# Gates of two chunks at a time by seven products of halves, from chunk 6 on

## The chip, the core and the metric

The kernel runs on one core of a Trainium2 chip. The metric is the device time of one execution in microseconds (us). The engines of the core are TensorE (PE, matmuls into PSUM; PEld is its loading of weights), VectorE (DVE), ScalarE (ACT), GpSimd (POOL) and SyncE (SP, which only issues DMAs here).

## What is computed

Linear attention with random features, and behind it a bilinear feed-forward layer on all 4608 tokens:

```
proj = q_s @ omega.T ; h = proj - |q_s|^2 / 2        # the same for k
q_p, k_p = exp(h - max(h)) / sqrt(m)                  # 128 features a head
kv = sum_s k_p^T v ; z = sum_s k_p                    # a batch and a head
x  = (q_p @ kv) / (q_p . z + 1e-6)                    # 4608 tokens x 512
out = ((x @ w1) * (x @ w2)) @ w3 @ w_out              # w1, w2 512 x 1024; w3 1024 x 1024; w_out 1024 x 512
```

All inputs are float32; 8 batches, 8 heads, 576 tokens a batch, head size 64.

## The kernel before

Tokens go in 36 chunks of 128. For each chunk the kernel makes k's features (`k_chunk`), q's features (`q_chunk`), q's attention (`q_attend`, whose result `xs` holds 128 tokens x 512), the transposed tokens for the gates (`x_turn`), the gates (`gate`) and the output (`project_out`). w3 and w_out are multiplied into one matrix `W` at the start (`W_block`), so the output is one product of the gated values with `W`.

Precision is kept by parts: a float32 operand is split into a high and a low fp16 half (`split`: ACT writes the high one, DVE or POOL the low one), and a product is the three passes high-high, high-low, low-high (`PASSES`). The first chunks are an exception: k and v of chunks below `VF` stay fp32 and are multiplied in one pass (`kv_batch`). The exponentials of q's features come in two forms, chosen by chunk in `DQ`: '1' takes eight ACT operations of one head each, with the maximum as their bias; '0' takes one DVE addition of 128 x 1024 and one ACT operation.

A gate (`gate`, lines 1191 to 1243) takes two chunks (256 tokens) from `GROUPS` on; the first four chunks go one by one. For each of 8 tiles of 128 of the 1024 columns it makes x @ w1 and x @ w2, each as 4 blocks of the 512 rows x 3 passes = 12 matmuls whose moving operand has 256 columns (128 for single chunks). Two tiles share a PSUM bank (`bank_m`, tag `pm`, 4 banks). ACT reads the first factor out (`asb`), DVE multiplies it with the second, ACT casts the high half into `big` and POOL makes the low half. The three pairs of chunks 28 to 33 (`LATE`) have another form behind the gate: `W` is cut into quarters, sums of quarters are mixed beforehand (`mix`, lines 1261 to 1301), DVE sums the gated parts, and `pair_first` and `pair_rest` make the output by seven products in place of eight.

What sets the order: all operations are recorded, in the order in which the code issues them, and then placed by a list scheduler (`Plan`), which knows each operation's inputs and outputs, a cost for each (`cost`, line 322), the buffers of a tag, and that POOL and DVE keep each other from SBUF in some forms (`locks`). It tries several rankings and keeps the best. Each engine then runs its own operations in the planned order, waiting on semaphores. PE operations of one bank and one kind are joined to groups of at most 24 matmuls (`JOIN`). Where the plan leaves PE idle in the first 200 us, `fill` puts matmuls on `ones_bf` that nobody reads.

Of the kernel before, what the change touches and what calls it, by code (L numbers as in the profile page):

```python
# [39 lines left out]
DQ = '1'  # L40
QF = 6
KF = 11
VF = 7
# [4 lines left out]
WADD = 1  # L48
# [12 lines left out]
LATE = 28  # L61
LATE_END = 34
MIX_N = 3
MIX_E = 'd'
SUM_E = 'd'
LO_E = 'p'
# [23 lines left out]
O_BUFS = 2  # L90
RAW_BUFS = 2
ASB_BUFS = 2
BIGS = 4
MAGS = 4
# [156 lines left out]
class Plan:  # L251
# [9 lines left out]
    def record(self, lane, method, args, kwargs):  # L261
# [15 lines left out]
        )  # L277
        if join:
# [43 lines left out]
    def cost(self, op):  # L322
# [20 lines left out]
        if op.lane == "vector":  # L343
# [5 lines left out]
            elif op.method == "tensor_reduce" or len(wide) > 1:  # L349
                t = 72 + 1.1 * m + (60 if thin else 0)  # L350
# [3 lines left out]
        if op.lane == "scalar":  # L354
            t = (130 if thin else 60) + 0.9 * m + (60 if "accum_out" in op.kwargs else 0)
# [3 lines left out]
        elif op.method == "tensor_tensor":  # L359
            t = 95 + 2.0 * m  # L360
# [119 lines left out]
    def order(self):  # L480
# [16 lines left out]
        plain = {o: set(o.deps) for o in ops}  # L497
        scale = TURN0
        for n in range(ROUNDS):
            start, total, slot = self.forward(rank, plain, turned(plain), costs, True, scale=scale)  # L500
# [3 lines left out]
            for m in range(INNER + 1):  # L504
# [3 lines left out]
                if best is None or total < best[0]:  # L508
                    best = total, start, slot
# [10 lines left out]
        _, start, slot = best  # L520
# [49 lines left out]
ROOM = {"big": 2050}  # L570
# [7 lines left out]
LOCK = True  # L578
HOP = 80
ROUNDS = 2  # L580
INNER = 2
# [4 lines left out]
def tile_favor_attention_then_bilinear_ffn(  # L586
# [35 lines left out]
    def early(kind, fn):  # L622
        return fn
# [53 lines left out]
    def power_of_two(cols, n, name, pre=1.0, add=False, bufs=4):  # L677
# [4 lines left out]
        if add:  # L682
            total = small("total")
# [120 lines left out]
    def features(c, name, e=None):  # L804
# [9 lines left out]
        def project(first=None):  # L814
            for i in range(NP):
                if whole(c, name):
                    for g in range(2):
                        d = slice(g * D, (g + 1) * D)
                        nc.tensor.matmul(
                            pg[:, g, i], raw[d, i], om_raw[d], start=first is None, stop=True  # L820
                        )
                    continue
                for n, (x, y) in enumerate(PASSES):
                    for g in range(2):
# [5 lines left out]
                            start=first is None and n == 0,  # L830
# [6 lines left out]
        nm = small("nm", H)  # L837
# [4 lines left out]
        if kind == "2":  # L842

            project(lambda h: nm[:, h : h + 1].broadcast_to([P, M]))
            nc.scalar.activation(e, pj, AF.Exp, scale=es, bias=ln_e)
        elif kind == "1":
# [106 lines left out]
    def q_attend(c):  # L953
# [7 lines left out]
        for h in range(H):  # L961
# [10 lines left out]
        gd = small("gd", H)  # L972
# [3 lines left out]
        gr = small("gr", H)  # L976
        nc.vector.reciprocal(gr, gd)
        xs = at.tile([P, HD], F32, tag="xs", name=f"xs_{c}", bufs=1)
        nc.vector.tensor_tensor(
            xs.rearrange("p (g i d) -> p g i d", g=2, d=D),  # L980
# [4 lines left out]
        mx = small("mx")  # L985
        nc.vector.tensor_reduce(mx, xs, AX.X, ALU.max, apply_absolute_value=True)
        xss[c] = xs, mx, owners

    def x_turn(c):

        xs, mx, owners = xss.pop(c)
        nc.vector.tensor_scalar(mx, mx, TINY, 2.0**-12, ALU.max, ALU.mult)
        p, r = pow2(mx, 1, f"x{c}")

        pt = sm.tile([P, 1], F32, tag="pt", name=f"pt_{c}", bufs=14)
        for b, r0, r1 in owners:
            nc.vector.tensor_scalar(pt[r0:r1], p[r0:r1], pv[b][r0:r1], None, ALU.mult)
        pts[c] = pt
        t = at.tile([P, 2, HD], F16, tag="xhl", name=f"xhl_{c}", bufs=1)
# [29 lines left out]
    for i in range(TOPS):  # L1029
        t = const.tile([P, 1024], F32, name=f"top_{i}")  # L1030
# [62 lines left out]
    def w12_split(n, i):  # L1093

        l1m = small("l1m")
# [4 lines left out]
        s = small("ws")  # L1100
# [23 lines left out]
    def W_block(n):  # L1124
# [8 lines left out]
        def product():  # L1133
            w = w3c[0].rearrange("p (j i) -> p j i", j=HALF)
            for k in range(2):
                ps = bank_m(f"wp_{n}_{k}")
                if j0 and not WADD:
                    nc.tensor.matmul(ps, ident, Wb[:, i + k + 1], start=True, stop=False)
                for j in range(HALF):
# [4 lines left out]
                        start=j == (0 if WADD else j0),  # L1144
# [46 lines left out]
    def gate(c0, n, u):  # L1191
# [20 lines left out]
        if LATE <= c0 < LATE_END:  # L1212
            g = at.tile([P, 8, P], F32, tag="ek", name=f"g_{c0}_{u}", bufs=EK_BUFS)
            asb = g[:, 0:4].rearrange("p b s -> p (b s)").rearrange("p (f s) -> p f s", f=nf)
            nc.scalar.mul(asb, ab[0], 2.0**-39)
            nc.vector.tensor_tensor(asb, ab[1], asb, ALU.mult)
            by = engine(SUM_E, u)
            by.tensor_tensor(
# [350 lines left out]
```

## Time and profile before

| | us |
|---|---|
| median of 3 runs (780.41 to 781.48) | 780.99 |
| the profiled execution | 780.73 |
| its span, first to last instruction | 779.0 |
| PE busy | 768.9 |
| DVE busy | 512.5 |
| ACT busy | 504.5 |
| POOL busy | 231.5 |

The mean granted PE clock is 0.997 of full speed. Busy time is the time covered by at least one of an engine's instructions. Matmuls are pipelined, so one lasts longer than the distance to the next one: from the start of a group to the start of the group behind it is the better measure of what it costs. Line numbers are of no help in this kernel, since one helper (line 173) issues everything; groups are told apart by the names of tiles and by shapes. `xT` are transposed tokens, `w12b` the split w1 and w2, `Wb` the output matrix, `big` the gated parts, `asb` gate values on the way, `hl` split q and k, `ek`/`eq` features, `vhl` split v, `mag` scratch.

### The profile page before, as it was taken

How to read it: one execution, taken by the hardware profiler on the slowest of the kernel's cores; microseconds unless marked ns; L12 is line 12 of the kernel's file. 1: busy time of each engine (PE TensorE's matmuls, PEld its weight loads, DVE VectorE, ACT ScalarE, POOL GpSimd, SP SyncE). 2: the span in 40 equal slices, each digit the busy share in tenths (PEclk: the TensorE clock that was granted, in tenths of full speed). 3: DMA queues.
4: the chain of work that ended last, by engine and by line, in shares of the span. 5: the costliest groups of instructions: out<-in, count | busy, mean ns of one | idle time of the engine just before them, and what ended most of it. 6: DMA issues, size and time to landing. Idle time of an engine off the chain costs nothing.

```text
span 779.0 us, 20533 instructions
## 1 busy us (share of the span) xinstructions
PE 768.9 (99%) x8525; PEld 591.0 (76%) x8533; DVE 512.5 (66%) x1093; ACT 504.5 (65%) x1038; POOL 231.5 (30%) x210
## 2 busy tenths in 40 slices
PE   9999999998999999999999999999999999999998
PEld 5456589877787777777777777777777777788886
DVE  4357989999764866676667666586668555865311
ACT  5899889756673858668666676587566546444221
POOL 1000020414252434324342334234432433433110
PEclk9999999999999999999999999999999999999999
DMA  9998983324533364263454435164442333322101
GB/s 332 364 308 304 195 169 64 83 56 123 123 83 69 66 179 93 60 162 83 83 102 130 96 83 115 41 149 97 74 101 49 76 80 72 69 42 69 41 2 55
DMA packets 142621, 88.43 MB, mean 114 GB/s; under 512 B 116736, under 2 KB 117120, under 8 KB 142528
## 3 DMA queue, kind: packets, MB, share of 16 engines
q1 hardware_dynamic: 142016, 86.07, 44.9%
q8 instruction: 67, 1.10, 0.6%
q10 hardware_dynamic: 432, 0.79, 0.3%
q14 instruction: 26, 0.21, 0.1%
q0 software_dynamic: 80, 0.26, 0.1%
HBM read 49.35 MB, written 9.44 MB: 75 GB/s over the span
## 4 chain that ended last, share of the span: by engine, by line
PE 87%; DVE 8%; ACT 3%; issue 1%; ACTq 0%; DVEq 0%
PE pm L173 73%; PE pa L173 14%; DVE mag L173 2%; ACT e L173 1%; DVE s_nm L173 1%; DVE Wb L173 1%; DVE w12b L173 1%; DVE vhl L173 1%; DVE hl L173 1%; ACT top L173 0%; ACT junk L173 0%; DVE ek L173 0%; DVE asb L173 0%; DVE xhl L173 0%; DVE xs L173 0%
## 5 line engine op out<-in xcount | busy, mean ns | idle before, releaser
L173 PE MATMUL pm<-xT,w12b 128*128 128x256 f16 (+1 forms) x3840 | 391.5, 262 | 0.4 <-DVE s_es L173 0.4
L173 PEld LDWEIGHTS <-w12b 128*128 128x128 f16 x3840 | 339.1, 98 | 38.1 <-issue 0.5
L173 PE MATMUL pm<-Wb,big 128*128 128x512 f16 (+1 forms) x852 | 173.9, 361 | 0.0
L173 PEld LDWEIGHTS <-big 128*128 128x128 f16 x996 | 95.9, 98 | 80.2 <-issue 1.6
L173 DVE TENSOR_REDUCE s_nm<-pa 128x8 f32<-128x1024 f32 x72 | 86.7, 1219 | 79.0 <-PE pa L173 78.5
L173 POOL TENSOR_TENSOR eq<-e,eq 128x1024 f16<-128x1024 f32 x31 | 67.5, 2177 | 197.1 <-issue 85.8
L173 POOL TENSOR_TENSOR big<-asb,big 128x512 f16<-128x512 f32 x60 | 78.0, 1299 | 160.5 <-ACT big L173 157.4
L173 ACT ACTIVATE e<-pa,s_nm,s_es 128x128 f32<-128x128 f32 x240 | 87.4, 468 | 30.7 <-DVE s_nm L173 19.5
L173 POOL TENSOR_TENSOR ek<-e,ek 128x1024 f16<-128x1024 f32 x26 | 56.4, 2169 | 56.2 <-ACT ek L173 45.5
L173 DVE TENSOR_TENSOR asb<-pm,asb 128x512 f32<-128x512 f32 x60 | 41.2, 686 | 45.7 <-PE pm L173 44.3
L173 ACT CAST big<-asb 128x512 f16<-128x512 f32 x60 | 37.7, 628 | 44.9 <-DVE asb L173 44.8
L173 ACT ACTIVATE o<-pm,oscs 128x512 f32<-128x512 f32 (+1 forms) x31 | 21.0, 676 | 64.0 <-PE pm L173 63.9
L173 PE MATMUL pm<-mag,mag 128*128 128x512 f32 x128 | 57.4, 598 | 0.4 <-DVE mag L173 0.4
L173 ACT ACTIVATE asb<-pm 128x512 f32<-128x512 f32 x60 | 36.2, 604 | 24.1 <-PE pm L173 22.7
L173 PE MATMUL pa<-om,hl 64*128 64x128 f16 x1320 | 44.3, 218 | 3.7 <-DVE hl L173 2.3
L173 PEld LDWEIGHTS <-hl 64*128 64x128 f16 x1320 | 37.4, 95 | 13.0 <-issue 8.2
L173 PEld LDWEIGHTS pm<-mag,mag 128*128 128x128 f32 x128 | 23.6, 190 | 27.0 <-issue 25.6
L173 DVE SCALAR_TENSOR_TENSOR xhl<-xs,s_p2r,xhl 128x512 f16<-128x512 f32 x36 | 32.3, 897 | 17.4 <-ACT xhl L173 17.2
L173 PE MATMUL pa<-vhl,ek 128*128 128x65 f16 (+1 forms) x896 | 43.2, 205 | 0.1
L173 DVE CAST eq<-e 128x1024 f16<-128x1024 f32 x30 | 21.0, 699 | 29.7 <-ACT e L173 21.3
L173 ACT ACTIVATE e<-e,ln_e,s_es 128x1024 f32<-128x1024 f32 x25 | 31.5, 1258 | 13.4 <-DVE e L173 13.4
L173 POOL TENSOR_TENSOR big<-ek,big 128x896 f16<-128x896 f32 x12 | 22.8, 1897 | 41.2 <-ACT big L173 41.2
(117 smaller groups left out, 933.7 us busy)
## 6 DMA issues: line engine op xcount, KB each, us to landing
vraw<-v SPq DMA_DIRECT2D x36, 256.0 KB, 4.4
qraw<-qT SPq DMA_DIRECT2D x35, 256.0 KB, 2.9
big<-w3T SPq DMA_DIRECT2D x8, 1024.0 KB, 9.0
big<-w SPq DMA_DIRECT2D x8, 1024.0 KB, 6.9
kraw<-kT SPq DMA_DIRECT2D x32, 256.0 KB, 2.8
out<-o SPq DMA_DIRECT2D x28, 256.0 KB, 2.2
big<-wo SPq DMA_DIRECT2D x3, 1024.0 KB, 6.8
out<-e SPq DMA_DIRECT2D x6, 256.0 KB, 2.1
```

What stands on the lines that cost most here:

```text
L173: p.real = getattr(lanes[p.lane], p.method)(*args, **{k: real(a) for k, a in p.kwargs.items()})
```

## The change

The gates of chunks 6 to 35 are made in 15 pairs by seven products in place of eight (`SG = 6`). The operand of a pair is seen as 2 x 2 blocks (two chunks x two halves of the 512 rows) and so are the weights of one half of the columns (two halves of the rows x w1 and w2, 512 columns each). Every product is 128 tokens x 256 x 512: 4 tiles x 2 blocks x 3 passes = 24 matmuls of 128 columns, and there are seven for each half `i`, in three recorded pieces:

```diff
+    def product(ps, m, i, x, fresh=False):
+        g, k = PIECE[m]
+        for f in range(4):
+            mm = [(cc, a, b) for cc in range(2) for a, b in PASSES]
+            for j, (cc, a, b) in enumerate(mm):
+                nc.tensor.matmul(
+                    ps[:, f * P : (f + 1) * P],
+                    factor(m, i, cc)[:, a, f * P : (f + 1) * P],
+                    x[g][:, b, 2 * k + cc],
+                    start=fresh and f == 0 and j == 0,
...
+    def pair_gate(c0, i):
...
         def first():
+            product(X, 1, i, x, True)
+            nc.scalar.mul(st["s1"], X, 2.0**-37)
+            product(X, 6, i, x)
+            nc.scalar.copy(st["u2"], X)
...
         def second():
+            product(Z, 5, i, x, True)
+            nc.scalar.copy(s5, Z)
+            product(X, 7, i, x)
+            nc.vector.tensor_tensor(s5, X, s5, ALU.add)
+            product(Z, 3, i, x)
+            nc.vector.tensor_tensor(u2, Z, u2, ALU.add)
...
         def third():
+            product(X, 4, i, x)
+            nc.vector.scalar_tensor_tensor(s5, X, 2.0**-37, s5, ALU.mult, ALU.mult)
+            Y = bank_m(f"Y_{c0}_{i}")
+            product(Y, 2, i, x, True)
+            nc.vector.scalar_tensor_tensor(s1, Y, 2.0**-37, s1, ALU.mult, ALU.add)
+            engine(H0_E, i).tensor_tensor(s1, s1, u2, ALU.mult)
+            in_halves(c0, i, s1)
+            in_halves(c0 + 1, i, s5)
```

The product that comes second in a bank adds onto what the first left there. The sums of weight parts for products 4 to 7 are made once, by DVE with ACT for the high halves (`mix`, four times 12 DVE operations of 128 x 512 and 4 ACT casts), into planned slots of `big` and `mag`; product 4's take the place of a block of `w12b`. The sums of token parts are made for each pair by POOL ahead of the transposes, which now go in two DMAs of 12 and 16 blocks a pair (16 blocks in two DMAs before):

```diff
+    def pair_turn(c):
+        x = pieces.pop(c - 1)
+        by = engine(SUM_E, 0)
+        by.tensor_tensor(x[:, 1], x[:, 4], x[:, 5], ALU.add)
+        by.tensor_tensor(x[:, 2], x[:, 1], x[:, 0], ALU.subtract)
+        by.tensor_tensor(x[:, 4], x[:, 0], x[:, 4], ALU.subtract)
+        by.tensor_tensor(x[:, 6], x[:, 3], x[:, 2], ALU.subtract)
...
+        for m, (a, b) in enumerate(((0, 3), (3, 7))):
...
+            nc.scalar.mul(hi, src, r)
+            nc.vector.scalar_tensor_tensor(lo, src, r, hi, ALU.mult, ALU.subtract)
...
+            nc.sync.dma_start_transpose(d, t)
```

The seven-product form of the output (`LATE`, `products`, `pair_first`, `pair_rest`, the old `mix`) is gone; chunks 28 to 33 go through `project_out`. Some choices and buffers are others, and the planner has other costs, ten more tries from a seeded random ranking, and no longer joins fp32 matmuls of 128 rows whose inputs come at different times:

```diff
-DQ = '1'
+DQ = '100110000'
...
-VF = 7
+VF = 2
...
-O_BUFS = 2
+O_BUFS = 1
...
-ASB_BUFS = 2
-BIGS = 4
-MAGS = 4
+ASB_BUFS = 3
+BIGS = 3
+MAGS = 6
...
+TRIES = 10
+SPREAD = 500.0
```

On PE the order of the changed kernel holds 5040 matmuls of 128 columns on pairs (2160 on `mag`, 2880 on `w12b`), 192 of 256 columns for chunks 4 and 5, 840 of 512 and 48 of 256 for the output, and 78 of 512 columns on `ones_bf` where there were 65.

ACT, in the last 100 us, before: `asb` and `ek` are gate factors read from a bank, `big` the high halves, `xhl` the split tokens, `hl` split q, `e` an exponential of one head (x8) or an output.

```order
L173 ACTIVATE ek5_484<-pm1_118 128x512
L173 ACTIVATE xhl0_110<-xs0_107,s_p2r1_42_721 128x512
L173 CAST big3_172<-ek5_484 128x896
L173 ACTIVATE ek0_86<-pm0_84 128x512
L173 COPY e1_622<-pm1_118 128x256
L173 CAST big3_172<-ek0_86 128x896
L173 ACTIVATE ek5_484<-pm0_84 128x512
L173 ACTIVATE xhl0_110<-xs0_107,s_p2r1_40_97 128x512
```

The same place after: `asb` from a bank is product 1, 6 or 5, `o` an output.

```order
L172 ACTIVATE asb1_432<-pm0_82 128x512
L172 COPY asb0_89<-pm2_118 128x512
L172 COPY asb2_538<-pm0_82 128x512
L172 ACTIVATE o0_79<-pm1_117,oscs_76 128x512
L172 CAST big2_165<-asb1_432 128x512
L172 CAST big2_165<-asb0_89 128x512
L172 ACTIVATE asb2_538<-pm3_373 128x512
L172 COPY asb0_89<-pm1_117 128x512
L172 COPY asb1_432<-pm3_373 128x512
```

One bank is now read twice in three rows (`pm0`, for products 1 and 6, with product 5 from `pm2` between), where before each reading was of another bank or of a bank filled anew.

DVE, where the changed weights are mixed ahead of the first pair, before: `mag` on `Wb` is the old mixing of the output matrix.

```order
L173 TENSOR_TENSOR mag3_370<-Wb_63,mag3_370 128x256
L173 TENSOR_TENSOR mag3_370<-mag3_370,Wb_63 128x256
L173 CAST ek4_364<-e1_622 128x1024
L173 TENSOR_TENSOR mag3_370<-mag3_370,Wb_63 128x256
L173 TENSOR_SCALAR pm1_118<-pm1_118 128x3
L173 TENSOR_TENSOR asb0_91<-pm2_308,asb0_91 128x512
```

After: `big` on `w12b` is a sum of weight parts, `w12b` on `big` the low half of product 4's.

```order
L172 TENSOR_TENSOR e1_315<-pa1_180,s_nm2_259 128x1024
L172 TENSOR_TENSOR big1_152<-big1_152,w12b_72 128x512
L172 SCALAR_TENSOR_TENSOR hl0_80<-kraw0_78,s_s3_42_2508,hl0_80 128x512
L172 TENSOR_TENSOR w12b_72<-big2_165,w12b_72 128x512
L172 CAST ek2_309<-e1_315 128x1024
L172 TENSOR_TENSOR w12b_72<-big1_152,w12b_72 128x512
L172 MEMSET vam0_88 128x8
L172 TENSOR_TENSOR big1_152<-w12b_72 128x512
```

Operations of 256 columns on the output matrix give way to operations of 512 on w1 and w2, and features of k and q of 1024 columns stand between them.

## Rows read from the trace of the kernel before

**Rows 1.** The page's first part: busy us (share of the span) xinstructions.
```profile
PE 768.9 (99%) x8525; PEld 591.0 (76%) x8533; DVE 512.5 (66%) x1093; ACT 504.5 (65%) x1038; POOL 231.5 (30%) x210
```

**Rows 2.** Stretches: us, busy of PE, PEld, DVE, ACT, POOL, clock, DMA, GB/s.
```profile
0.00:140.00 140.00, 137.56 (x1221) 92.27 (x1230) 97.05 (x205) 120.91 (x267) 10.71 (x35) 1.00 0.84 242
140.00:180.00 40.00, 39.62 (x547) 30.32 (x545) 38.89 (x86) 26.74 (x54) 15.61 (x7) 1.00 0.36 88
180.00:220.00 40.00, 36.67 (x418) 29.42 (x417) 32.02 (x67) 26.86 (x60) 15.64 (x10) 0.96 0.45 107
460.00:500.00 40.00, 40.00 (x531) 31.35 (x530) 24.86 (x49) 23.47 (x47) 13.67 (x18) 1.00 0.35 81
```

**Rows 3.** Groups by form: engine, operation, shapes, count | busy us, mean ns | idle.
```profile
L173 PE MATMUL pm<-xT,w12b 128*128 128x256 f16 x3072 | 346.6, 273 | 0.0
L173 PE MATMUL pa<-vhl,ek 128*128 128x65 f16 x768 | 29.6, 193 | 0.0
L173 PE MATMUL pa<-vhl,ek 128*128 128x65 f32 x128 | 16.0, 276 | 0.1
L173 PEld LDWEIGHTS <-w12b 128*128 128x128 f16 x3840 | 339.1, 98 | 38.1 <-issue 0.5 <-DMA xT<-xhl 0.4
```

**Rows 4.** PE in order of time: start us, length us, operation, count.
```profile
136.95 9.56 PE L173 MATMUL pm<-xT,w12b 128*128 128x128 f16 x168
146.45 1.16 PE L173 MATMUL pa<-om_raw,kraw 64*128 64x128 f32 x16
...
170.18 1.50 PE L173 MATMUL pm<-xT,w12b 128*128 128x128 f16 x24 [0.38 <-DVE s_es L173]
171.51 5.34 PE L173 MATMUL pm<-Wb,big 128*128 128x512 f16 x24
176.69 1.50 PE L173 MATMUL pm<-xT,w12b 128*128 128x128 f16 x24
...
179.58 5.42 PE L173 MATMUL pm<-xT,w12b 128*128 128x256 f16 x48
184.83 0.17 PE L173 MATMUL pm<-sums,ones_bf 128*128 128x3 bf16 x1
```

**Rows 5.** Groups by form on DVE, ACT and POOL, columns as in rows 3.
```profile
L173 DVE TENSOR_TENSOR asb<-pm,asb 128x512 f32<-128x512 f32 x60 | 41.2, 686 | 45.7 <-PE pm L173 44.3 <-ACT xhl L173 0.9 <-ACT asb L173 0.4
L173 DVE TENSOR_TENSOR e<-pa,s_nm 128x1024 f32<-128x1024 f32 x26 | 31.6, 1217 | 0.8 <-POOL ek L173 0.3
L173 DVE SCALAR_TENSOR_TENSOR w12b<-w12b,s_ws 128x512 f16<-128x512 f32 x16 | 11.9, 742 | 2.7 <-ACT w12b L173 2.6
L173 DVE TENSOR_TENSOR mag<-mag,Wb 128x256 f32<-128x256 f32 x28 | 12.7, 480 | 0.0
...
L173 ACT ACTIVATE e<-e,ln_e,s_es 128x1024 f32<-128x1024 f32 x25 | 31.5, 1258 | 13.4 <-DVE e L173 13.4
...
L173 POOL TENSOR_TENSOR big<-asb,big 128x512 f16<-128x512 f32 x60 | 78.0, 1299 | 160.5 <-ACT big L173 157.4 <-DVE vhl L173 3.1
```

**Rows 6.** Tile asb, 220 to 660 us: operations, and idle us, times, before them.
```profile
L173 DVE TENSOR_TENSOR asb<-pm,asb x44: 675/690/692, 222.2 to 625.4; 128x512 f32<-128x512 f32 x44
...
L173 ACT ACTIVATE asb<-pm x43: 570/597/640, 226.7 to 622.9; 128x512 f32<-128x512 f32 x43
...
  PE pm L173: 34.6, 29
```

**Rows 7.** A bank is left and read: PE and DVE in order of time.
```profile
759.63 2.78 PE L173 MATMUL pm<-ek,big 128*128 128x256 f16 x24
759.90 0.69 DVE L173 TENSOR_TENSOR asb<-pm,asb 128x512 f32<-128x512 f32 x1 [4.55 <-PE pm L173]
```

**Rows 8.** PE waits for DVE: POOL, DVE and PE in order of time.
```profile
191.88 2.12 POOL L173 TENSOR_TENSOR eq<-e,eq 128x1024 f16<-128x1024 f32 x1 [0.68 <-POOL ek L173]
192.03 2.52 DVE L173 SCALAR_TENSOR_TENSOR hl<-qraw,s_s,hl 128x512 f16<-128x512 f32 x1 [0.28 <-ACT hl L173]
194.61 1.25 PE L173 MATMUL pa<-om,hl 64*128 64x128 f16 x20 [2.27 <-DVE hl L173]
195.79 6.38 PE L173 MATMUL pm<-Wb,big 128*128 128x512 f16 x24
```

More of the change, by code (lines that the diff above doesn't have):

```diff
@@ L277, in record @@
         )
+        if join and SPLIT and op.ins[0].dtype == F32 and rows(op) == 128:
+            join = not any(
+                other not in prior.deps and other is not prior
+                for b in ins
+                for other, o in self.writes.get(b[0], [])
+                if self.meet(b, o)
+            )
         if join:
@@ L829, in project @@
                             om[d, y],
-                            start=first is None and n == 0,
+                            start=n == 0,
                             stop=n == len(PASSES) - 1,
@@ L1243, in gate @@
                 hs[c0 + t, u * nf + k] = h[:, :, k, t * P : (t + 1) * P]
[L1246 to L1255 removed]
+        if c0 + n == SG and (u + 1) * nf == NF:
+            for _ in mix_work:
+                pass
     def engine(kinds, i):
@@ L1317, in pair_first @@
[L1317 to L1339 removed]
+    mixed, pair, half = {}, [], [0]
@@ new lines, in mix, with parts @@
+    def mix(i, cc):
+        b11, b12, b21, b22 = (w12[n][i][cc + 2 * k] for k in range(2) for n in range(2))
+        by = engine(MIX_E, 2 * i + cc)
+        t = at.tile([P, 3, 512], F32, tag="big", name=f"mix_{i}_{cc}", bufs=BIGS)
+        p, q, r = (t[:, n] for n in range(3))
+        def parts(n, t):
+            if n == 4:
+                d = w12[1][i][cc]
+            else:
+                if half[0] % 2 == 0:
+                    pair.append(at.tile([P, 2, 512], F32, tag="mag", name=f"mixed_{n}_{i}_{cc}", bufs=MAGS))
+                d = halves(pair[-1][:, half[0] % 2])
+                half[0] += 1
+            mixed[n, i, cc] = d
+            nc.scalar.copy(d[:, 0], t)
+            by.tensor_tensor(d[:, 1], t, d[:, 0], ALU.subtract)
+        yield by.tensor_tensor(p, b12[:, 0], b12[:, 1], ALU.add)
+        yield by.tensor_tensor(q, p, b11[:, 0], ALU.subtract)
+        yield by.tensor_tensor(q, q, b11[:, 1], ALU.subtract)
+        yield parts(5, q)
+        yield by.tensor_tensor(r, b22[:, 0], b22[:, 1], ALU.add)
+        yield by.tensor_tensor(p, r, p, ALU.subtract)
+        yield parts(7, p)
+        yield by.tensor_tensor(r, r, q, ALU.subtract)
+        yield parts(6, r)
+        yield by.tensor_tensor(q, b21[:, 0], r, ALU.subtract)
+        yield by.tensor_tensor(q, q, b21[:, 1], ALU.add)
+        yield parts(4, q)
@@ new lines, in mixes, with factor @@
+    def mixes():
+        for i in range(2):
+            for cc in range(2):
+                yield from mix(i, cc)
+    mix_work = mixes()
+    def factor(m, i, cc):
+        if m in (1, 2):
+            return w12[0][i][cc + 2 * (m - 1)]
+        return w12[1][i][cc + 2] if m == 3 else mixed[m, i, cc]
+    PIECE = {1: (0, 0), 5: (0, 1), 6: (0, 2), 2: (1, 0), 7: (1, 1), 4: (1, 2), 3: (1, 3)}
+    def product(ps, m, i, x, fresh=False):
[8 more added lines that the diff above has]
+                    start=fresh and f == 0 and j == 0,
+                    stop=f == 3 and j == len(mm) - 1,
+                    skip_group_check=True,
+                )
@@ new lines, in temp, with in_halves @@
+    def temp(name):
+        return mo.tile([P, 512], F32, tag="asb", name=name, bufs=ASB_BUFS)
+    def in_halves(c, i, t):
+        c0 = c - (c - SG) % 2
+        if c0 not in parts:
+            parts[c0] = at.tile([P, 4, 512], F32, tag="big", name=f"h_{c0}", bufs=BIGS)
+        h = parts[c0][:, 2 * (c - c0) + i].bitcast(F16).rearrange("p (x f s) -> p x f s", x=2, f=4)
+        d = h.rearrange("p x f s -> p x (f s)")
+        nc.scalar.copy(d[:, 0], t)
+        nc.gpsimd.tensor_tensor(d[:, 1], t, d[:, 0], ALU.subtract)
+        for f in range(4):
+            hs[c, 4 * i + f] = h[:, :, f]
```

247 lines of the change are left out of this document (100 added, 147 removed).

## Prediction

> **What bounds the kernel now.** I read the page first, then the stretches, then the forms and single rows of TensorE (PE). PE is busy 768.9 us of a span of 779.0, the other three between 231.5 and 512.5 [rows 1]. The stretches say where this is tight: in 460 to 500 us PE fills all 40.00 us at clock 1.00 while VectorE (DVE) has 24.86, and in 180 to 220 PE misses 3.3 us [rows 2]. So from about 220 us on the time is the sum of PE's work, and a matmul column less is time less, as long as nobody makes PE wait. The profiled execution took 780.73 us, 1.7 around its span; the median is 780.99. My sum is made on 780.73.
>
> **PE's work, part by part.** I take durations from start to start, since the busy time of a group counts the overlapping tails. A change of the gates touches 30 chunks, 15 pairs.
>
> Gates. A pair now takes 8 tiles x 2 factors x 12 = 192 matmuls of 256 columns; 48 of these lie between 179.58 and 184.83, so 109.4 ns each [rows 4]. Removed: 2880 x 109.4 = 315.0 us, 15/16 of the 3072 in [rows 3]. Added: 2 halves x 7 products x 24 = 336 matmuls of 128 columns a pair, 5040 in all (the changed order counts 2160 on the mixed parts and 2880 on `w12b`). The same form runs today in chunks 0 to 3: 24 of them take 1.33 us (170.18 to 171.51), 55.4 ns each; the longest unbroken row, 168 from 136.95 to 146.45, gives 56.5 with the change to a 64-row form at its end [rows 4]. I take 55.7, nearer to the single groups: 280.7 us. Gain 34.3, by the two rows 30.2 to 35.8. It is on the path in full, all after 190 us.
>
> Outputs. The three pairs that had seven quarter products in the output go back to the plain form: 252 matmuls of 256 columns leave (27.6 us), 144 of 512 columns come, at 5.18 us for 24 (171.51 to 176.69) [rows 4], 31.1 us. Loss 3.5.
>
> k^T v. With `VF` 2 instead of 7, 48 fp32 matmuls become 144 in fp16. The trace lists each fp32 one twice: 128 records, 64 matmuls, 16.0 us, so 250 ns; fp16 29.6 / 768 = 38.5 ns, three of them 116 [rows 3]. Gain 48 x 0.134 = 6.4 us. All of it lies before 140 us, where PE also waits for loads; the order has 13 more filler matmuls of 512 columns there (2.8 us at 216 ns), which says that less than the half is lost again. I count 6.4 - 2.8 = 3.6; between 0 and 6.4.
>
> Sum of PE's work: -34.3 + 3.5 - 3.6 = -34.4 us.
>
> **The other engines, as work.** DVE gets 60 scalar_tensor_tensor and 12 tensor_tensor more on gate results (0.686 by the nearest row), 33 additions of 1024 for q's features (1.217), and 48 operations of 512 for the mixed weights (0.742 by the nearest row, the weight split) [rows 5]: 49 + 40 + 36 = 125 us. It loses 56 operations of 256 of the old mixing (0.480, 27 us) and, in the old output form, some 60 more of 128 to 512 columns (at the same 0.480, 29 us). So DVE goes from 512 to about 580 us, under 80% of the span. ScalarE (ACT) gives up eight exponentials a chunk for one of 1.258 [rows 5] and gets 42 more evictions, and stays about where it is. GpSimd (POOL) has 231.5; 60 additions of 256 have no row and lie between half of 1.299 and the whole, and 30 of 512 at 1.299 [rows 5]: 78 to 117 us more, less 12 of the old form; near 310. As totals these hide behind PE. Two places decide whether they do in time. (DMA: a pair's transposes grow from 16 to 28 blocks on SP, and two of the three `xT` buffers are now one pair's. The order reads a pair's second tile some 17 us of PE work after the older tile in its buffer was last read; I price this at nothing, and with that cover gone, at the transpose's landing, a few us per pair.)
>
> **Hand-offs of a bank.** Product 6 adds onto product 1 in the same bank, so it may start only when ACT has read product 1 out; likewise 7 after 6, 3 after 5, and 4 after DVE's read of 7. What is queued behind a waiting matmul is all of PE. In the order before, at least 4 us of other PE work (by the paces above) lay between a bank's last matmul and its next user wherever it was read in between. After, I count 29 hand-offs with a single group of 24 between, 1.33 us, and 18 with about 2. The price of one: a gate group is left at 759.63, DVE starts to read at 759.90 and needs 0.69 [rows 7], and PE starts 0.06 us after a DVE operation that it waits for (192.03 + 2.52, then 194.61) [rows 8]; 0.27 + 0.69 + 0.06 = 1.02 us, 0.93 with ACT's 0.597 [rows 6]. So 1.33 is enough by 0.3 to 0.4 us if the reading engine is free at once. Today it is often not: of 87 evictions in 220 to 660 us only 29 found their engine waiting for PE [rows 6]. The longest operation in front is an exponential of 1.258 us [rows 5]; half of one costs 0.63 - 0.35 = 0.3 us, so 29 x 2/3 x 0.3 = 5.6 us, and 0 if the order puts the evictions first. 19 of the 29 stand in the last 100 us, where the order shows ACT only evictions, casts of 0.6 us and outputs, so I take 4.
>
> **The mixed weights.** They must be made between the weight split and the first pair, near 213 us. On top of the old mixing DVE has there 36 - 27 = 9 us, 9 for parts of k and v that are now split (3 x 1.217 + 6 x 0.742 and a cast), and 7 for six q chunks (1.217 each) [rows 5]: 25 us more before 220. DVE has 1.1 us free in 140 to 180 and 8.0 in 180 to 220, but 43 before 140 [rows 2]. The order starts the first mix ahead of the last weight conversions, and the k and v parts lie earlier still, so most goes into the 43. What does not fit delays PE: between 0 and 16 us. Nearest is 0, and I take 1.5. If PE waits here it costs twice: after the gap of 2.27 us at 194.61 the next 24 outputs took 6.38 us [rows 8] against 5.34 [rows 4], with the clock at 0.96 over that stretch [rows 2].
>
> Forecast: 780.73 - 34.4 + 4 + 1.5 = 751.8, **752.0**. With free hand-offs and all of k^T v: 780.7 - 37.2 = 743.5.
>
> **Rivals.** *Weight loads bind (slower).* Each matmul of 128 columns brings its own weight load, whose mean is 98 ns [rows 3], longer than the 55.7 ns of the matmul. If loads hide only behind longer matmuls once such groups follow each other for 500 us, every matmul costs more. The gain is gone at 55.7 + 28.7/5040 us = 61.4 ns; at 98 ns the time would be 752 + 213 = 965. Against it: 168 in a row at 56.5 ns with the loads in between [rows 4]. For it: only 4 x 192 = 768 such matmuls run today, in stretches of at most 10 us. The Trainium skill (TensorE: Matmul & The Clock Gate, Part 2, Back-to-back issue gap) says that in a stream of weight loads and matmuls both set the spacing, about 81 ns at 128 columns; by that rule the time, as an estimate, is 752 + 5040 x 0.0253 = 880. The trace disagrees with it here: 55.4 to 56.5 ns.
>
> *Late readers.* Evictions stand behind a whole exponential: 29 x 2/3 x 0.9 = 17 us instead of 4, time 765. For it: 58 of 87 start behind other work today. Against: the order is planned with these waits in it, and 19 hand-offs lie where no exponential is left.
>
> *Late mixes.* DVE, with POOL beside it (2.52 us for an operation that the nearest row has at 0.742 [rows 5], while POOL ran 2.12 us [rows 8]), delivers the parts 15 us late, plus 2 for the clock: 767. For it: DVE is full in 140 to 180. Against: 43 us free before.
>
> That the change does not do what it says is excluded by the order: the 128-column matmuls are there, and the 256-column ones are down to one pair's 192 and the last output's 48.
>
> **How the numbers follow.** Forecast and its neighbourhood 744 to 759: 0.68. Late readers 0.14, late mixes 0.08, better than 744 0.04, weight loads 0.06. The range 744 to 767 takes in the first three, some 0.85. 0.2% is 1.6 us, about what a measurement of this kernel tells from no change. Faster 0.92, same 0.02, slower 0.06.
>
> **What would show it.** PE's group of 128 columns at 55 to 57 ns from start to start and PE busy near 99% of a span near 750: the sum holds. Waits "PE pm <- ACT asb" or "DVE asb" of some 4 us in all: hand-offs as priced; over 12, late readers. A gap or a clock under 1.00 between 200 and 250 us with DVE at 39 of 40: late mixes. Wrong altogether if the pace is over 61 ns.

## The result, and the profile after

The changed kernel takes 767.64 us (median of 4 runs, 766.92 to 771.24) against 780.7 us before, a ratio of 0.985 (95% interval 0.982 to 0.988). Faster, as forecast, but by 13 us where I had said 29: the time lies just above my range. A repeat beside the experiments gave 770.03 us (767.2 to 771.18) and a ratio of 0.989 (0.986 to 0.992). The page of the changed kernel, to be read against [rows 1] (second line: tenths of 40 slices of 19.2 us):

```profile
span 769.5 us, 24572 instructions
...
PE 744.6 (97%) x10640; PEld 580.4 (75%) x10646; DVE 583.9 (76%) x1078; ACT 481.4 (63%) x838; POOL 319.4 (42%) x306
...
DVE  4659999999999999999899999969774644522120
```

PE's busy time fell by 24.3 us and its idle time rose from 10.1 to 24.9 us. DVE's total is what I forecast (about 580), but see where it lies: nine tenths or more in nearly every slice from 60 to 500 us, and little after. The same in stretches, the kernel before first, then the changed one (start and end, length, then busy us and instructions of PE, PEld, DVE, ACT, POOL, and PE's granted clock):

```profile
140.00:220.00 80.00, 76.29 (x963) 59.73 (x961) 70.91 (x152) 53.60 (x113) 31.26 (x17) 0.98 0.41 97
220.00:500.00 280.00, 279.59 (x3321) 215.92 (x3320) 183.91 (x384) 185.96 (x375) 102.89 (x100) 1.00 0.43 98
500.00:740.00 240.00, 240.00 (x2729) 193.87 (x2727) 155.41 (x347) 136.51 (x273) 82.00 (x55) 1.00 0.36 76
```

```profile
140.00:220.00 80.00, 77.79 (x1079) 62.11 (x1080) 78.62 (x143) 56.30 (x100) 32.86 (x21) 1.00 0.46 103
220.00:500.00 280.00, 270.60 (x4555) 223.06 (x4553) 267.63 (x483) 203.64 (x338) 170.62 (x156) 0.99 0.61 125
500.00:740.00 240.00, 234.82 (x3470) 189.50 (x3467) 123.05 (x238) 93.59 (x141) 99.06 (x88) 1.00 0.34 68
```

From 220 to 500 us DVE went from 183.9 to 267.6 of 280 us, and POOL from 102.9 to 170.6; from 500 to 740 DVE lost 32. PE, which had missed 0.4 us in both together, now misses 9.4 and 5.2. What it waits for (waits of PE in all, number, longest):

```profile
PE pm L172 <- ACT asb L172: 6.5, 8, 2.0
PE pa L172 <- DVE e L172: 6.0, 6, 2.4
PE pm L172 <- DVE asb L172: 1.7, 2, 1.5
PE pa L172 <- DMA eqT<-eq: 1.5, 2, 0.8
PE pm L172 <- DMA xT<-xhl: 1.3, 1, 1.3
```

Two kinds, then: banks that ACT or DVE reads out late (8.2 us), and features that DVE makes late (6.0; `pa` is free again only when DVE has made `e` from it). The longest of the second kind, with what went before (PE's, DVE's and POOL's rows in order of time: start, length, what, and in brackets the idle time ahead):

```profile
473.85 0.84 PE L172 MATMUL pa<-om,hl 64*128 64x128 f16 x24
477.08 1.48 PE L172 MATMUL pa<-kv,eqT 128*128 128x65 f16 x24 [2.39 <-DVE e L172]
...
478.43 2.44 PE L172 MATMUL pm<-xT,mag 128*128 128x128 f16 x24
...
470.36 2.88 DVE L172 SCALAR_TENSOR_TENSOR xhl<-xs,s_p2r,xhl 128x768 f16<-128x768 f32 x1
473.17 1.40 DVE L172 SCALAR_TENSOR_TENSOR vhl<-vraw,s_s,vhl 128x512 f16<-128x512 f32 x2
474.49 1.21 DVE L172 TENSOR_REDUCE s_nm<-pa 128x8 f32<-128x1024 f32 x1
475.81 1.23 DVE L172 TENSOR_TENSOR e<-pa,s_nm 128x1024 f32<-128x1024 f32 x1
...
469.85 2.58 POOL L172 TENSOR_TENSOR ek<-e,ek 128x1024 f16<-128x1024 f32 x1
```

DVE's operation on `xhl` lasts 2.88 us beside POOL's; in the repeat, the five of the same form with no POOL row beside them take 1.01 on the mean. DVE has no gap in which to make that up, and 1.5 us after its end PE begins to wait, for 2.39 us. The group of 24 behind it took 2.28 us (478.43 to the next start at 480.71) in place of 1.34: the granted clock was 0.50, the lower of its two levels, in 478.40 to 479.60 us, and 0.96 over 460 to 500.

The pace of the gates in undisturbed rows is what I took it for. Three rows of PE:

```profile
314.94 1.50 PE L172 MATMUL pm<-xT,w12b 128*128 128x128 f16 x24
316.28 1.50 PE L172 MATMUL pm<-xT,mag 128*128 128x128 f16 x24
317.71 0.84 PE L172 MATMUL pa<-om,hl 64*128 64x128 f16 x24
```

1.34 us for 24, 55.8 ns each, on split weights and on mixed ones, with a weight load for every one; 1.43 where a form of 64 rows follows.

### The profile page after: what moved, and what is told of

It reads as the page before. It is cut to its first block, busy times and chain, and to the rows that moved or that the text cites. A ratio compares the mean times of both kernels' runs of the same rounds, so it can differ in the third digit from the quotient of the medians.

```text
span 769.5 us, 24572 instructions
## 1 busy us (share of the span) xinstructions
PE 744.6 (97%) x10640; PEld 580.4 (75%) x10646; DVE 583.9 (76%) x1078; ACT 481.4 (63%) x838; POOL 319.4 (42%) x306
## 4 chain that ended last, share of the span: by engine, by line
PE 46%; DVE 33%; ACT 7%; DMA 6%; issue 5%; POOL 1%; SPq 0%; DVEq 0%; ACTq 0%; POOLq 0%
PE pm L172 40%; PE pa L172 6%; DVE s_nm L172 4%; DMA xT<-xhl 4%; DVE e L172 4%; DVE asb L172 4%; DVE hl L172 3%; DVE xhl L172 3%; DVE vhl L172 3%; DVE big L172 2%; ACT e L172 1%; DVE xs L172 1%; DVE s_mx L172 1%; DVE mag L172 1%; DMA eqT<-eq 1%
## 5 line engine op out<-in xcount | busy, mean ns | idle before, releaser
L172 PE MATMUL pm<-xT,w12b 128*128 128x128 f16 (+1 forms) x3840 | 244.4, 222 | 1.6 <-DMA xT<-xhl 1.3
L172 PEld LDWEIGHTS <-w12b 128*128 128x128 f16 x3840 | 226.8, 98 | 10.2 <-issue 2.4
L172 PE MATMUL pm<-xT,mag 128*128 128x128 f16 x2160 | 134.0, 220 | 6.2 <-ACT asb L172 6.0
L172 PEld LDWEIGHTS <-mag 128*128 128x128 f16 x2160 | 124.3, 98 | 9.5 <-issue 7.2
L172 DVE SCALAR_TENSOR_TENSOR asb<-pm,asb 128x512 f32<-128x512 f32 x60 | 40.6, 680 | 60.3 <-PE pm L172 60.3
L172 ACT ACTIVATE e<-e,ln_e,s_es 128x1024 f32<-128x1024 f32 x55 | 67.6, 1237 | 29.1 <-DVE e L172 28.6
L172 POOL TENSOR_TENSOR asb<-asb,asb 128x512 f32<-128x512 f32 x30 | 40.3, 1342 | 108.3 <-DVE asb L172 107.6
L172 DVE TENSOR_TENSOR e<-pa,s_nm 128x1024 f32<-128x1024 f32 x59 | 71.2, 1213 | 0.6
L172 DVE SCALAR_TENSOR_TENSOR xhl<-xs,s_p2r,xhl 128x768 f16<-128x768 f32 (+2 forms) x36 | 47.5, 1323 | 22.2 <-ACT xhl L172 22.2
L172 POOL TENSOR_TENSOR xs<-xs 128x256 f32<-128x256 f32 x60 | 48.6, 828 | 7.6 <-DVE xs L172 6.7
```

Of the source, the lines that this page charges most:

```text
L172: p.real = getattr(lanes[p.lane], p.method)(*args, **{k: real(a) for k, a in p.kwargs.items()})
```

## The experiments

Theory F: DVE is full from 60 to 500 us, so what delays it reaches PE. Theory H: the banks are passed on too soon. Later came A (ACT itself is late) and C (POOL stretches DVE's operations). Two more names, L and W, are told where they come up. Ratios are against the kernel before, run beside each of them.

### The kernel again, and its parts

`e0_after`, no edit. 

> The changed kernel as it is, beside the experiments on the same chip, and for a second profile. Both theories: 767 to 768 us, TensorE waits of some 14 us after 220 us, VectorE busy 37 to 39 of every 40 us from 220 to 500. Where the first profile's two stretches at clock 0.96 are chance, this one has none and its span is 3 us shorter.

Ratio 0.989 (above). Its profile has a span of 765.4 us, no stretch from 60 us to 740 under clock 1.00, and the same waits (ACT `asb` 5.9, DVE `e` 5.9, DVE `asb` 1.4). It is the fastest of the repeat's four runs (767.2 us), so gains counted from its span are at the small end. I make sums on this one; its stretches:

```profile
140.00:220.00 80.00, 77.97 (x1084) 62.40 (x1085) 78.62 (x147) 56.31 (x101) 33.19 (x21) 1.00 0.47 104
220.00:500.00 280.00, 271.18 (x4623) 223.58 (x4620) 267.72 (x497) 206.72 (x342) 174.51 (x157) 1.00 0.63 127
500.00:740.00 240.00, 234.85 (x3455) 189.03 (x3453) 118.43 (x221) 92.18 (x139) 94.94 (x86) 1.00 0.33 67
```

`e4_none`:

```diff
-SG = 6
+SG = 36
-        if c0 + n == SG and (u + 1) * nf == NF:
-            for _ in mix_work:
-                pass
```

> The changed kernel with no pair by seven products: all pairs by the old 256-column form, no mixed weights, all other edits (exponentials, k^T v, buffers, costs, ten tries) kept, the seven-product output still gone. By the starts of TensorE's groups the gates cost 26.6 us more, and both theories take back the waits of some 10 us: 767.6 + 26.6 - 10 = 784 us. If it is 781 the other edits are worth nothing beside the 3.5 us that the lost output form costs; at 775 the seven products are worth 8 us only and the rest of the gain belongs to the other edits.

777.85 us, ratio 0.998 (0.997 to 0.999), between the times that I had named. The other edits are worth 0.2%, with the lost output form in them, the seven products some 0.9 to 1.3% of 780, 7 to 10 us. (This kernel is planned anew, so a part of that can be its order.) Without them DVE has room and PE next to no waits after 220 us:

```profile
220.00:500.00 280.00, 279.93 (x3391) 216.44 (x3389) 193.96 (x387) 164.30 (x274) 101.54 (x99) 1.00 0.42 99
500.00:740.00 240.00, 239.93 (x2587) 185.27 (x2585) 140.16 (x284) 107.28 (x169) 74.92 (x56) 1.00 0.34 74
```

PE is busy 767.3 us here and 741.7 in the repeat, so the seven products take 25.6 us of work off PE, and PE's idle time (9.0 against 23.7 us) takes 14.7 of that back, where I had counted 10.

### Two rough tests

`e1_dq1` (`DQ = '1'`, planned anew). 

> One choice of the change undone: q's exponentials as eight ScalarE operations a chunk again, as before, with no addition on VectorE. Theory F (VectorE is full from 60 to 500 us, so that what delays it reaches TensorE): VectorE loses some 33 x 1.2 = 40 us, two thirds of the 14 us of TensorE's waits after 220 us go, 759 us (756 to 763). Theory H (a bank is passed on after one group of 24 matmuls, 1.33 us, and its reader, mostly ScalarE, is late by one operation): ScalarE gains 33 x (8 x 0.47 - 1.24) = 83 us, its evictions come later, 772 us or more.

775.81 us, 0.995 (0.994 to 0.997): what H had said, and F's 759 is far off. But it is not ACT that reads late: waits for its evictions cost less (3.2 us), those for DVE's readings of banks more (7.1 us against 1.4). DVE is hardly less busy (576.2 us), though 33 additions are gone: by the tally told under `e8_pool`, its operations are stretched beside POOL by 59.6 us in this order, by 32.3 in the repeat. The largest wait, 5.28 us at 226 us, is for mixed weights (DVE's and POOL's rows, in order of time):

```profile
226.00 0.19 PE L172 MATMUL pm<-sums,ones_bf 128*128 128x3 bf16 x1 [5.28 <-ACT mag L172]
...
218.70 2.20 DVE L172 TENSOR_SCALAR s_nm<-s_nm,s_es 128x8 f32<-128x8 f32 x1
220.81 0.68 DVE L172 TENSOR_TENSOR big<-big,w12b 128x512 f32<-128x512 f32 x1
221.41 1.64 DVE L172 TENSOR_TENSOR big<-w12b,big 128x512 f32<-128x512 f16 x1
...
218.75 2.12 POOL L172 TENSOR_TENSOR ek<-e,ek 128x1024 f16<-128x1024 f32 x1
220.83 3.23 POOL L172 TENSOR_TENSOR big<-asb,big 128x512 f16<-128x512 f32 x2
```

An operation of eight columns takes 2.20 us: it ends 0.03 us after POOL's. So this run relieved DVE of little and tests a new order more than a theory, and it shows POOL and DVE in each other's way.

`e5_lat`:

```diff
-            return t, 170, work * rows(op) / 128
+            return t, 700, work * rows(op) / 128
```

> Only the planner's belief is changed: results of TensorE count as ready 0.70 us after the end of a group in place of 0.17. In the order that it makes no bank is passed on behind a single group of 24 any more (29 before), 19 behind some 2 us. Theory H: the waits for readers of banks (7.9 us after 220 us) fall under 3 us, 762 us (760 to 764). Theory F: VectorE is as full as before and what it delays reaches TensorE at other places; 767 us (765 to 770).

768.14 us, 0.987 (0.984 to 0.990), as F said; yet H is seen at work. After 500 us, where the repeat loses 5.2 us, this order loses nothing; before 500 it loses more, above all in 140 to 220:

```profile
140.00:220.00 80.00, 75.12 (x967) 59.40 (x965) 78.59 (x136) 51.59 (x94) 32.01 (x21) 0.98 0.42 99
220.00:500.00 280.00, 269.30 (x4551) 221.10 (x4547) 267.51 (x488) 203.30 (x341) 169.38 (x154) 0.99 0.60 124
500.00:740.00 240.00, 240.00 (x3612) 194.87 (x3611) 126.26 (x236) 97.77 (x148) 98.28 (x89) 1.00 0.36 71
```

So short hand-offs cost some 4 us where DVE is free: of the 5.2 us, 3.9 are waits for readers of banks, the rest for `e` and `eqT`. Where DVE is full, the waits in this order only moved.

### One engine relieved at a time, in the same order

In the next three runs the planner's search is replaced by the start times and buffer numbers that it had found, so that every engine keeps its order, and one engine gets less to do.

`e6_dve`:

```diff
-        nc.vector.tensor_reduce(nm, pj, AX.X, ALU.max, negate=True)
+        nc.vector.tensor_reduce(nm, pj[:, :, 0 : M // 4], AX.X, ALU.max, negate=True)
...
```

> Every engine's order and every buffer as in the changed kernel; only VectorE has less to do: the maximum of the projections is taken over a quarter of the features (256 of 1024 values; the rest is left out, and the exponentials' offset is lowered so that nothing overflows). 72 reductions of 1.21 us become some 0.35 us: 62 us less on VectorE, most of it in 60 to 600 us. Theory F (VectorE is full from 60 to 500 us, and what delays it reaches TensorE): of the 10.7 us that TensorE waited in 140 to 500 us (profile of the repeated changed kernel) under 3.5 stay; 759 us (757 to 761). Theory H (banks are passed on too soon and ScalarE reads them out late): the waits for ScalarE's readings, 5.9 us, stay as they are, and only the 6 us for features go; 763 to 764 us.

756.76 us, 0.970 (0.969 to 0.972): F, to 2 us, though more of PE's idle time in 140 to 500 us stays than I had said (5.4 of 10.9 us). The 72 reductions went from 87.3 to 30.0 us. A rival reading is that these maxima stand in the chain that frees `pa` (maximum, then `e`), so that a shorter chain helps and not a freer DVE. `e8_pool`, below, leaves them at 1.21 us and gains as much, and `e4_none` had them with DVE at 194 of 280 us and no waits.

`e7_act`:

```diff
+        if len(src.shape) > 2:
+            q = src.shape[2] // 4
+            dst, src = dst[:, :, 0:q], src[:, :, 0:q]
         nc.scalar.activation(dst, src, AF.Square, scale=pre, accum_out=out)
```

> The same order and buffers, and ScalarE has less to do: the sums of squares of q, k and v are taken over a quarter of the values (128 of 512; the rest is left out, so scales are other powers of two). 95 operations of 0.63 us become some 0.3 us: 31 us less on ScalarE, all before 600 us. Theory F: TensorE's waits stay within 2 us, 766 us (765 to 768). Theory A (ScalarE itself is what comes late: its evictions stand behind other work of its own): the 5.9 us of waits for its readings of banks fall under 3, 763 to 764 us.

767.13 us, 0.984 (0.982 to 0.985). ACT is 28 us less busy and nothing follows; A falls.

`e8_pool`:

```diff
-        (nc.vector if lo == "d" else nc.gpsimd).tensor_tensor(t[:, 1], e, t[:, 0], ALU.subtract)
...
+            nc.gpsimd.tensor_scalar(t[:, 1], t[:, 0], 2.0**-13, 1.0, ALU.mult, ALU.mult)
```

> The same order and buffers, and GpSimd has less to do: the low halves of the features of q and k are made by an operation with one input in place of two (what it writes is not the low half; the subtraction is left out). 59 operations of 2.2 us become some 1.1 us: 60 us less on GpSimd. Theory C (VectorE is full because GpSimd beside it stretches its operations, as in 2.61 us for one of 0.76 us): VectorE's rows add up to at least 10 us less, TensorE's waits fall by half, 761 us (759 to 763). Theory F without C: VectorE's rows fall by under 4 us, 766 us (765 to 768).

756.85 us, 0.970 (0.968 to 0.972): more than C had hoped. The three in 220 to 500 us, `e6_dve`, `e7_act` and `e8_pool` in turn:

```profile
220.00:500.00 280.00, 276.62 (x4719) 228.16 (x4719) 245.53 (x501) 210.06 (x350) 177.19 (x160) 1.00 0.64 129
```

```profile
220.00:500.00 280.00, 271.54 (x4602) 224.02 (x4600) 267.35 (x493) 187.76 (x340) 174.22 (x156) 0.99 0.63 127
```

```profile
220.00:500.00 280.00, 277.51 (x4727) 228.51 (x4725) 260.52 (x498) 208.46 (x347) 135.81 (x158) 1.00 0.65 129
```

PE misses 3.4, 8.5 and 2.5 us where the repeat misses 8.8. Relief of DVE by 51 us (rows of all its operations, 645 to 594) or of POOL by 67 us is worth the same, 10.4 and 10.3 us of span. In `e8_pool` DVE's rows add up to 13 us less, with not one operation taken from it. That POOL's own results come sooner is not what helps: the waits on transposes of what POOL writes (`eqT`, `xT`) go from 2.9 to 2.4 us, those for `e` of DVE and for ACT's readings from 11.8 to 4.8. Why 13 us of DVE's time are worth as much here as 51 in `e6_dve` stays open.

Which operations POOL stretches is seen row by row. I took all of DVE's operations that overlap one of POOL, and subtracted the median of those of the same form that do not. In the repeat this gives 32.3 us (36.8 in the first profile of the same order, so a few us are chance; the 22.6 in expectations below counts only a part of the rows), nearly all on forms whose inputs lie in SBUF: `hl` of q 1.04 us (15 operations) against 0.74 (15), `xhl` of 768 columns 1.49 (10) against 1.01 (5), the cast `eq` of one input 0.91 (12) against 0.68 (18). Forms that read PSUM show nothing: `asb` 0.68 and 0.68, `e` 1.21 and 1.21. The reduction `s_mx` of one SBUF operand shows nothing either (0.68 and 0.68). In `e8_pool` the sum is 19.3 us: the 13 us that DVE's rows lost are this stretch. The Trainium skill (SBUF — State Buffer, SBUF: two separate sides) says that VectorE and GpSimd take turns on one pair of ports for whole instructions, that a VectorE operation needs the pair in a two-port mode, or with two SBUF inputs beside a GpSimd operation that reads SBUF, and that the loser blocks until the other is through. The rows agree: the operation of eight columns in `e1_dq1` that took 2.20 us ended with POOL's.

### New orders with work moved between engines

Each is planned anew. `e9_qh` (`QH` all `'a'`: 30 casts of `eq` from DVE to ACT). 

> A complete kernel: the high halves of q's features are all cast by ScalarE (the first six chunks are so already), 30 casts of 0.77 us off VectorE, 30 of 1.06 us onto ScalarE, planned anew. Theory F: 23 us of relief for VectorE in its full stretch take 4 us of TensorE's waits, 763 us (761 to 766). Theories A and H: ScalarE with 32 us more reads its banks later, 770 us or more.

770.6 us, 0.988 (0.985 to 0.990): no gain, and the figure of A and H. Yet the waits for ACT's readings fall to 4.0 us; those for DVE's rise to 6.9, one of them 4.2.

`e2_seed2` (`SEED = 2`). 

> A complete kernel: the changed one with another seed for the planner's ten tries, so the same operations in another order. It tells how much of a difference between two orders is luck. All theories: within 4 us of 767.6; VectorE as full in 60 to 500 us.

770.03 us, 0.987 (0.983 to 0.990): the same operations in another order, as far off as expected.

`e10_sumd` (`SUM_E = 'd'`). 

> A complete kernel: the sums of token parts (60 additions of 128 x 256 a run) go from GpSimd to VectorE. Theory F alone (the work on VectorE counts): VectorE gets some 60 x 0.34 = 20 us more in its full stretch, 771 us or more. Theory C (GpSimd and VectorE keep each other waiting in operations that have all inputs in SBUF; in the profile of the changed kernel such VectorE operations are 22.6 us longer beside GpSimd than alone): GpSimd loses 50 us; taking 67 us off it with VectorE as it was saved 10.5 us, so -8 us, and +4 for the 20 us on VectorE (51 us less there saved 10.5): 763 us (761 to 766).

779.98 us, 1.000 (0.998 to 1.002): the whole gain gone, 9 us above the least that F alone had said and 17 above C. DVE is near full up to 580 us, PE misses 15.6 us in 220 to 500, and the granted clock falls to 0.98 there:

```profile
220.00:500.00 280.00, 264.43 (x4517) 220.24 (x4514) 271.34 (x507) 197.95 (x328) 135.10 (x116) 0.98 0.58 120
500.00:740.00 240.00, 237.80 (x3564) 193.06 (x3563) 148.22 (x275) 103.00 (x159) 87.65 (x69) 1.00 0.35 74
```

`e11_bothd` (with `H0_E = 'd'` as well). 

> A complete kernel: beside the sums of token parts also the product of the first chunk's two factors (30 multiplications of 128 x 512) goes from GpSimd to VectorE: GpSimd -90 us, VectorE some +40. Theory F: 775 us. Theory C: -14 + 8, 762 us (759 to 766).

769.73 us, 0.985 (0.982 to 0.989). Between F (775) and C (762).

`e13_sumd_lat` (`SUM_E = 'd'`, and 500 in place of 170 in the cost). 

> A complete kernel: token sums on VectorE, and the planner believes results of TensorE ready 0.50 us after a group's end in place of 0.17; 18 hand-offs behind a single group instead of 28. If the two causes add up (the short hand-offs cost 5 us after 500 us, as the order with 0.70 showed), 759 us (757 to 763); if the planner only moves the waits, as the token sums alone, 763 us.

778.43 us, 0.998 (0.996 to 0.999), far above both figures (759 and 763).

None of the five is better than the changed kernel (767.6 and 770.0); what loads DVE more is the same or worse. `e11_bothd` gives DVE 30 operations more than `e10_sumd` and is 10 us faster. What the order does to DVE differs: beside POOL its operations are stretched by 56.1 us in `e10_sumd` and by 31.3 in `e11_bothd`, so that its rows add up to 692.8 and 689.0 us. The clock differs too (0.98 and 1.00 in 220 to 500 us). How much of the 10 us is the order, and how much the product that moved, is not shown; the two kernels with the same operations in another order, `e2_seed2` and `e5_lat`, lie within 2.5 us of the changed kernel. So runs with new orders can't weigh DVE's work against POOL's.

### GpSimd's operations cut, in the same order

Order, buffers and work stay; one POOL operation becomes two or four on parts of the columns. `e14_cut2` and `e15_cut4`, the low halves of the features in two and in four:

```diff
-        (nc.vector if lo == "d" else nc.gpsimd).tensor_tensor(t[:, 1], e, t[:, 0], ALU.subtract)
...
+            in_cuts(2, nc.gpsimd.tensor_tensor, H, t[:, 1], e, t[:, 0], ALU.subtract)
```

> A complete kernel in the order and the buffers of the changed one; each of GpSimd's 59 subtractions of 1024 columns (2.2 us, low halves of the features) is made as two of 512. Theory L (VectorE's operations that read only SBUF stand behind a long GpSimd operation, up to 2.6 us for 0.74; what counts is how long GpSimd keeps on at a stretch): the 22.6 us by which they are longer beside GpSimd fall under 14, and with VectorE full that gives 4 to 6 us: 762 us (760 to 765). Theory W (what counts is GpSimd's total, which stays or grows a little): 767 to 769 us.

> The same with four operations of 256 columns each, some 0.6 to 0.8 us long (the token sums of that size take 0.83). Theory L: no VectorE operation waits more than 0.8 us; excess under 9 us, 760 us (758 to 764). Theory W: GpSimd's total grows by some 59 x 4 x 0.1 = 24 us, 770 us.

767.15 us, 0.984 (0.982 to 0.986), and 766.86 us, 0.983 (0.980 to 0.986): no effect, and not what L had said. The stretch of DVE's operations is 30.6 and 28.9 us, where the repeat has 32.3; a split of 0.74 us on DVE still takes up to 1.76. Put down to the POOL operation that overlaps most, half of the repeat's stretch stands beside operations on the features (15.5 us), the other beside those of the gates and the token sums (17.1). With the features in four it is 8.3 and 22.3: what the cut takes away in one place comes back in the other.

`e16_cutall` (features and gates in two), `e17_gate2` (gates alone), `e18_gate4` (gates in four, features in two):

```diff
-            engine(H0_E, i).tensor_tensor(s1, s1, u2, ALU.mult)
+            in_cuts(2, engine(H0_E, i).tensor_tensor, 512, s1, s1, u2, ALU.mult)
...
-        nc.gpsimd.tensor_tensor(d[:, 1], t, d[:, 0], ALU.subtract)
+        in_cuts(2, nc.gpsimd.tensor_tensor, 512, d[:, 1], t, d[:, 0], ALU.subtract)
```

> As with two operations of 512 columns, and GpSimd's low halves of the gated values and products of factors (128 x 512, 1.24 and 1.34 us) are made as two of 256 columns. Theory L: excess under 11 us, 760 us (758 to 764). Theory W: 769 us. If the halves of the gated values are on the way to the outputs, their extra 0.2 us each costs at most 1 us in either.

> A complete kernel in the order of the changed one; only GpSimd's operations behind the gates (60 low halves of the gated values and 30 products of factors, 128 x 512) are made as two of 256 columns, those on the features stay whole. If the gates' operations alone do it (cutting the features' alone did nothing): 763 us (761 to 764). If it takes both cuts together: 766 to 767 us.

> A complete kernel in the order of the changed one; the same operations behind the gates as four of 128 columns, the features' as two of 512. Theory L (the length of one GpSimd operation): VectorE's excess falls further, under 14 us, 760 us (758 to 762). Theory W (GpSimd's total counts as well): 90 more operations x 2 x 0.15 us = some 27 us more on GpSimd, gain eaten up, 763 to 766 us.

762.44 us, 0.978 (0.976 to 0.981); 764.05 us, 0.979 (0.977 to 0.981); 771.55 us, 0.988 (0.985 to 0.990). `e16_cutall` is the fastest complete kernel of the study, faster than both given ones. Its stretch, and that of `e18_gate4`:

```profile
220.00:500.00 280.00, 274.95 (x4713) 227.48 (x4711) 268.27 (x505) 209.44 (x346) 196.15 (x240) 1.00 0.62 128
```

```profile
220.00:500.00 280.00, 270.94 (x4585) 223.04 (x4582) 261.33 (x492) 204.78 (x340) 208.61 (x318) 0.99 0.59 126
```

The gates' operations do it, in two parts. The stretch is 26.6, 27.9 and 22.9 us, so L's sums (under 11 for `e16_cutall`, under 14 for `e18_gate4`) fail. In four parts the stretch is the least, and yet the time is above both theories: POOL is busy 386.6 us against 319.5, and the waits for ACT's readings of banks grow to 8.3 us. That POOL's extra work eats the gain is likely and not shown. Theory L, that only the length counts, doesn't explain either result, nor why the features' cut gave nothing. That stays open.

`e19_latcut` (the order of `e5_lat` with the cuts of `e16_cutall`). 

> A complete kernel: the order planned with results of TensorE 0.70 us later (no hand-off behind a single group, 768.1 us as it was), with the features' and the gates' operations of GpSimd as two each. If the two causes add up, 768.1 - 5.2 = 763 us, and less (759 to 761) if the waits of that order before 500 us are those of a VectorE held up by GpSimd; if the cut only helped the short hand-offs, 767 us.

765.88 us, 0.983 (0.980 to 0.985), some 2 us less than `e5_lat`, where the cuts took 5 off the changed kernel. The gains do not add up in full.

## Why the prediction was wrong

On the repeat (span 765.4 us against 779.0) the account is:

| | forecast | measured |
|---|---|---|
| gates, PE's work | -34.3 | -28.8 |
| rest of PE's work | -0.1 | +1.6 |
| PE waits for readers of banks | +4 | +7.3 |
| PE's other idle time | +1.5 | +6.3 |
| span | -28.9 | -13.6 |

The first line is the sum of distances from row to row of PE, idle time left out: 336.9 + 43.6 before, 21.3 + 207.3 + 123.2 in the repeat. The second is the rest of PE's busy time (768.9 to 741.7), the fourth the rest of its idle time (10.1 to 23.7). Of the 15.3 us by which the forecast gained too much, 8.1 are idle time and 7.2 are PE's work.

**The step that failed** is "As totals these hide behind PE". DVE's total was right, 580 us; comparing it with the span was wrong. What the change adds on DVE goes with every pair; what it removes lay before 220 us (the old mixing) and at the end (the old output form). So DVE gained 84 us in 220 to 500 us and lost 32 in 500 to 740. A tally by stage would have warned me: DVE had 183.9 of 280 us in that stretch, and half of the 89 us that I counted for gates and q's features makes 228, 82%, with nothing yet for features that come sooner as PE gets faster, or for POOL. By the repeat's rows in that stretch the additions `e` grew by 27.9 us, the gate results by 18.6, the maxima by 10.6 (37 in place of 28, as features come sooner) and the stretch beside POOL by 9.2. `e6_dve` shows the price, 10.4 us of span. PE's idle time is 14.8 us there, and 15.1 in `e8_pool`, where my forecast comes to 15.6 (10.1 + 5.5): with the full engine relieved, the waits are as forecast, and what is left of the miss is PE's work. The same step missed POOL: I added its 78 to 117 us to its own total alone, though [rows 8] held the case of a DVE operation that lasted 2.52 us beside POOL. I used that row only for the mixing. `e8_pool` shows 10.3 us; since both relieve the same full engine, the two are not to be added.

**Hand-offs.** Mechanism right, size short: 7.3 us (8.2 in the first profile) against 4. The 19 of the last 100 us are as harmless as I argued (0.6 us in the repeat); the price was paid earlier, 1.9 us on ACT's readings and 1.4 on one of DVE's between 500 and 660 us, the rest before. `e5_lat` shows that an order without them has no idle time there. Before 500 us such an order only moves the waits. That ACT is the reader in most of them is not because ACT has much to do: 28 us less work on it took the waits for it from 5.9 to 5.2 us, 67 us less on POOL to 2.5.

**Gates.** A second step was mis-sized. The term of 280.7 us was too small by 6.2, and that of 315.0 by 0.6. The body pace is as taken (1.34 us for 24), but the mean over all 5808 matmuls of the form is 56.9 ns. Most of it is seen: 0.10 us in each of 29 changes to 64-row forms, 0.16 in each of 10 groups ahead of a wait (1.50 in place of 1.34). I took the pace of undisturbed rows for work that stands between other forms. In the rest of PE's work the outputs cost 1.8 us more (3.5 forecast) and k^T v with the fillers 2.8 less (3.6 forecast); some 3 us more lie in small forms that the change did not touch.

**Transposes.** I had priced the shared `xT` buffers at nothing, "a few us per pair" with the cover gone; one wait of 1.3 us (1.6 in the repeat) was there, so the term was small, though not nothing.

**Rivals.** Weight loads do not bind: 55.8 ns. (The 81 ns of the Trainium skill, TensorE: Matmul & The Clock Gate, Part 2, Back-to-back issue gap, are not seen here: groups of 24 that neither wait nor meet a change of form take 1.34 us.) Late readers (765) and late mixes (767) gave times near the measured one by luck; neither is what happened. 140 to 220 us, where the mixes are made, loses less than before (2.2 us against 3.7), and the waits for readers are half of the 17 us of that case. My sign for late mixes was met in the first profile all the same: DVE at 39.45 of 40 us in 200 to 240, the clock at 0.96, and a wait of 2.0 us at 223, with a mixing operation of 2.61 us beside POOL just before it. In the repeat DVE is as full there and neither the gap nor the clock is seen, so the case is worth some 4 us at most. In `e1_dq1` it occurs, with 5.28 us. The true case, a full DVE over 300 us, was not among my rivals. My list of signs had "DVE at 39 of 40" only for 200 to 250 us.

## What to carry to other kernels

Tally an engine's added and removed work by stage, not in total: an engine at 76% of the span can be full for 400 us of it, and then delays on it reach the engine that bounds. To find which engine is late, freeze the order and make one engine's work smaller at a time; in a planned kernel a new order also changes which operations meet on POOL and DVE (a stretch of 31 to 60 us in the orders here). Where VectorE and GpSimd both work on SBUF, count a part of GpSimd's time against VectorE as well (here VectorE lost 32 us beside 330 us of GpSimd's operations).

## What the runs showed of the hardware

A wait of PE is not always followed by a slower clock. In the changed kernel's profile a wait of 2.39 us at 477 us was, with the clock at its lower level right behind it (0.96 over 460 to 500 us); in the repeat the same wait was not (1.00 over 440 to 520):

```profile
474.94 0.90 PE L172 MATMUL pa<-kv,eqT 128*128 128x65 f16 x24 [2.40 <-DVE e L172]
475.70 1.50 PE L172 MATMUL pm<-xT,mag 128*128 128x128 f16 x24
477.04 1.50 PE L172 MATMUL pm<-xT,w12b 128*128 128x128 f16 x24
```

Here the 24 took 1.34 us (475.70 to 477.04). And GpSimd pays for cuts: a subtraction of 1024 columns took 2.31 us, of 512 columns 1.27, of 256 columns 0.75, so a quarter of the columns costs a third of the time.
